# The first tick of the first pair in two parts of channels, and two filter copies moved to ScalarE

## The chip, the cores and the metric

The kernel runs on one core of a Trainium2 chip. Its work is done by five engines that run beside each other and wait for each other through semaphores: TensorE (PE in the profile, PEld for its weight loads), VectorE (DVE), ScalarE (ACT), GpSimd (POOL) and SyncE (SP). The last two mostly issue DMAs here. The metric is the time of one execution on the device in microseconds; shown is the median of several runs.

## The reference

Two steps are computed, on an input of 8 sequences, 5696 positions and 128 channels. First a causal convolution of every channel with a filter as long as the sequence, through a Fourier transform of twice the length. Then a mixing in frequency space: 64 modes of the result are multiplied by complex 128x128 matrices, transformed back and added, and a last 128x128 product with a ReLU is added to that.

```python
L = 2 * S
Xf = np.fft.rfft(x, n=L, axis=1)
Hf = np.fft.rfft(h, n=L, axis=0)
y = np.fft.irfft(Xf * Hf[None], n=L, axis=1)[:, :S, :]      # the convolution
X = np.fft.rfft(y, axis=1)[:, :64]
Y[:, :64] = X mixed by w_r + i w_i                           # 128x128 for each mode
u = y + np.fft.irfft(Y, n=S, axis=1)
out = u + np.maximum(u @ w_ch, 0.0)
```

## The kernel before, in words

The length 5696 is split into 89 times 64, so that each Fourier transform becomes two matrix products. The eight sequences are taken as four pairs (`g_` from 0 to 3); both sequences of a pair lie beside each other in 64 partitions each.

For a pair, the **first transform** comes as 32 tiles of four channels each (`a_tile`, line 462). PE writes a tile into two PSUM banks, and ScalarE or VectorE copies it out to the array `As` (tile token `("as", j)`); the last tile, 31, is copied half by each. The **second transform** (`second`, line 608) takes the 90 frequencies in 23 ticks of four, and writes one bank for each of the two sequences, all 128 channels of four frequencies in a bank. It takes the channels from `d0` to `d1`: with all of them it reads all tiles of `As`, with fewer it reads the tiles up to `d1` alone. The **products** with the filter (`products`, line 628) are made by VectorE into the buffers `U`. Normally ScalarE first copies the two banks into `Xs` (`copied`, line 588), and VectorE multiplies from there. Tick 0 has a form of its own: the first sequence is multiplied straight from PSUM, and the second is copied first by ScalarE (`copy_b`) and then multiplied (`first_u`, line 620). Two ticks behind, PE transforms `U` back (`Z`, matmuls with `Wc`, two of three banks 4, 5, 6 in turn), ScalarE copies it out and SP's queue stores it to DRAM; three ticks behind, PE adds up the modes in bank 7 (matmuls with `G`).

The **filter** goes through the same second transform, but once only, in the stage of the first pair. `filter_tick` (line 487) makes four frequencies of it in two banks, an engine copies them to `Hs`, and two DMAs on SP's queue write a copy with both halves of the partitions exchanged. Filter ticks 0 to 5 are spread among the tiles of the first transform (lines 739 to 743). From then on tick `t` of the first pair makes filter tick `t + 6`, in banks 2 and 3, as the last thing that the tick puts on PE (line 733). Line 503 says which engine copies a filter tick: ScalarE for ticks 0, 1, 3, 4 and 5, VectorE for all others.

The order of work on each engine is the order in which these functions are called, and each engine follows it strictly; waits are worked out from tokens (tiles, banks, buffers) by a recorder. Three calls of `keep` put matmuls on PE whose results nobody reads: 16 between the last tile of the first transform and tick 0 of the first pair (line 744), and 8 after each of ticks 0 and 1 of that pair (line 752).

Tick 0 lies in banks 6 and 7 in all pairs (`ZSLOT`, line 602). In the pairs from the second on, its second transform is already done in two parts. The first 116 channels (`DA`) of both sequences are put on PE right after the last tile of the first transform (line 765); the other 12 follow in tick 0 for the second sequence (line 646) and in tick 1 for the first sequence (lines 678 to 680). The first pair does it in one piece, at the beginning of tick 0 (line 677).

Of the kernel before, what the change touches and what calls it, by code (L numbers as in the profile page):

```python
# [123 lines left out]
def bass_long_conv_fft__then__afno_spectral_mix_kernel(nc, x, h, moe_w_r, moe_w_i, moe_w_ch, out):  # L124
    B, S, D = x.shape
# [25 lines left out]
    c, s = np.cos(th), np.sin(th)  # L151
# [137 lines left out]
    ps = nc.alloc_psum_tensor("ps", [P, 8 * 512], F32)  # L289
# [9 lines left out]
    def bank(i):  # L299
        return ("bank", i)  # L300
# [123 lines left out]

    W1, W2, WI = wc_sb[:, 0:P], wc_sb[:, P:2 * P], wi_sb[:, :]
    XSLOT = [0, 2]
    ZSLOT, DA = 6, 116
    ZBANK = [4, 5, 6]
    MB = 7
    WARM = 92  # L430
# [56 lines left out]
    def filter_tick(t, banks):  # L487
        n = len(ticks[t])
        hb = banks
        for i, k in enumerate(ticks[t]):  # L490
            for r in range(2):
                for dh in range(2):
                    mm(pv(hb[dh], i * DH, [[1, DH]]),
                       ap(m_sb, MW, J * dh, J, k * 3 * J + (J if r == 0 else 0) + dh * J, [[1, P]]),
                       ap(ah_sb, HW, J * dh, J, (2 * k + r) * DH, [[1, DH]]), r == 0, r == 1,
                       AHT + mtok(k) + [("ag", k)], [bank(hb[dh])])
        lo, hi = KT * t * D, (KT * t + n) * D
        old = once("xr", [t_ for r_ in XR for t_ in r_]) if t == 0 else []
        for i in range(NXH):
            if KT * t + n > KH[i // 2]:  # L500
                old = old + once(("xh", i), xtok(i))
        evac(h_sb[:, lo:hi], pv(hb[0], 0, [[DH, n], [512, 2], [1, DH]]), [bank(hb[0]), bank(hb[1])], [("h", t, 0)],
             eng="scalar" if t < LH and t != 2 else "vector",
             after=old)
        for p0, p1 in ((0, J), (J, 0)):
            dma("sync", h_sb[p0:p0 + J, HW + lo:HW + hi], h_sb[p1:p1 + J, lo:hi], "s", [("h", t, 0)], [("h", t, 1, p0)])
        if t % 2 and t // 2 < NG:
            s0, s1 = t // 2 * GP, min(t // 2 * GP + GP, NS)
            dma("sync", g_sb[:, s0 * P:s1 * P], bass.AP(c_g, s0 * P, [[GW, P], [1, (s1 - s0) * P]]), "c", (),
                [("g", t // 2)], after=[("ag", k) for k in range(s0, s1)])  # L510
# [90 lines left out]
    def slot_of(g_, t):  # L601
        if t == 0:
            return ZSLOT
        if g_ == 0:
            return XSLOT[(t + 1) % 2 if not with_h_at(g_, t) else 0]
        return XSLOT[((t - 1) // 4 + t) % 2]
# [13 lines left out]
    def first_u(b, s_, row, tok, d0, d1):  # L620
        n = len(ticks[0])
        R.add("vector", lambda e: e.tensor_tensor(  # L622
            bass.AP(u_s[0], b * 512 + d0, [[2048, P], [1024, 2], [D, n], [1, d1 - d0]]),
            bass.AP(s_[0], s_[1] + d0, [[row, P], [0, 2], [D, n], [1, d1 - d0]]),
            bass.AP(h_sb, d0, [[2 * HW, P], [HW, 2], [D, n], [1, d1 - d0]]), MULT),
              [tok, ("h", 0, 0), ("h", 0, 1, 0), ("h", 0, 1, J)], [("u", 0)])

    def products(g_, t, sl):
        n = len(ticks[t])
        bk = [bank(sl), bank(sl + 1)]  # L630
        i = t % NU
        hv = bass.AP(h_sb, KT * t * D, [[2 * HW, P], [HW, 2], [0, 2], [1, n * D]])
        uv = bass.AP(u_s[i], 0, [[2048, P], [1024, 2], [512, 2], [1, n * D]])
        src = pv(sl, 0, [[0, 2], [512, 2], [1, n * D]])
        if t == 0:
            e = turns("e", list(range(NXS)))
            def copy_b():
                evac(bass.AP(x_s[e], 512, [[1024, P], [1, n * D]]), pv(sl + 1, 0, [[1, n * D]]), [bank(sl + 1)], [("xs", e)], eng="scalar")

            if g_ == 0:  # L640
                copy_b()
                first_u(0, (ps, sl * 512), 4096, bank(sl), 0, D)
                first_u(1, (x_s[e], 512), 1024, ("xs", e), 0, D)
                return
            first_u(0, (ps, sl * 512), 4096, bank(sl), 0, DA)
            second(g_, 0, DA, D, (1,))
            copy_b()
            first_u(1, (x_s[e], 512), 1024, ("xs", e), 0, D)
            return
        if not straight(g_, t):  # L650
            e = onchip.get((g_, t))
            if e is None:
                e = copied(g_, t, sl)
            src, bk = bass.AP(x_s[e], 0, [[1024, P], [0, 2], [512, 2], [1, n * D]]), [("xs", e)]
        R.add("vector", lambda e: e.tensor_tensor(uv, src, hv, MULT),  # L655
              bk + [("h", t, 0), ("h", t, 1, 0), ("h", t, 1, J)], [("u", i)])
# [10 lines left out]
    def tick(g_, t):  # L667
        if g_ + 1 < NP:
            for i in range(2 * XC):
                if t == XPLACE[g_ > 0][i]:  # L670
                    x_place(i, bass.AP(x_room(g_ + 1, i), 0, [[XB, NQ], [D, XN], [1, D]]), xtok(i))
        with_h = with_h_at(g_, t)
        if t < NT:
            of_two = t > 0 and twin(g_, t - 1)
            if not of_two:
                if g_ == 0 or t:
                    second(g_, t)
                if g_ and t == 1:
                    second(g_, 0, DA, D, (0,))
                    first_u(0, (ps, slot_of(g_, 0) * 512), 4096, bank(slot_of(g_, 0)), DA, D)  # L680
            products(g_, t, slot_of(g_, t))
            if twin(g_, t):
                second(g_, t + 1)
                if straight(g_, t):
                    copied(g_, t + 1, slot_of(g_, t + 1))
        drain = list(border[t]) if t in border and g_ + 1 < NP else []
        if drain and t >= NT:
            j, sl, e = drain.pop(0)
            a_tile(j, [sl], e)
        if g_ + 1 < NP:  # L690
            i = t // 2 - 1 if t % 2 == 0 else -1
            if g_ == 0:
                i = XLATE.index(t) + NXH if t in XLATE else -1
            if 0 <= i < 2 * XC:
                x_load(g_ + 1, i, x_room(g_ + 1, i), xtok(i), [("u", t % NU)] + AST)
        if LC <= t < NT + LC:
            s_ = t - LC
            n = len(ticks[s_])
            i, zi = s_ % NU, zroom(g_, s_)
            zb = [turns("z", ZBANK) for b in range(2)]  # L700
            for b in range(2):
                for r in range(2):
                    mm(pv(zb[b], 0, [[1, n * D]]), (W1, W2)[r], u_s[i][:, r * 1024 + b * 512:r * 1024 + b * 512 + n * D],
                       r == 0, r == 1, [("u", i), ("wc",)], [bank(zb[b])])
                evac(bass.AP(z_s[zi], b * D, [[1024, P], [2 * D, n], [1, D]]),
                     pv(zb[b], 0, [[D, n], [1, D]]), [bank(zb[b])], [("zs", zi, b)], eng="scalar",
                     after=once(("zx", zi, b), Z_OLD) if zi >= NZ else ())
            zo = (g_ * NK + KT * s_) * P * 256
            dma("sync", bass.AP(zs, zo, [[256, P], [P * 256, n], [1, 256]]),
                bass.AP(z_s[zi], 0, [[1024, P], [256, n], [1, 256]]), "z",  # L710
                [("zs", zi, 0), ("zs", zi, 1)], [("zd", g_, s_)])
            if drain and t >= NT:
                j, sl, e = drain.pop(0)
                a_tile(j, [sl], e)
        if LM <= t < NT + LM:
            s_ = t - LM
            zi = zroom(g_, s_)
            for i, k in sorted(enumerate(ticks[s_]), key=lambda q: (s_ > 0 or q[1] != 1, q)):
                for b in range(2):
                    if k % 2:  # L720
                        o, off, n, sl = pv(MB, b * P, [[1, P]]), (k + 1) // 2 * P, P, (k + 1) // 2
                    else:
                        ms, off = even[k]
                        n, sl = 2 * len(ms), 0
                        dims = [[M, 2]] if len(ms) == 1 else [[ms[1] - ms[0], 2], [M, 2]]
                        o = pv(MB, b * P + ms[0], dims)
                    mm(o, z_s[zi][:, i * 256 + b * P:i * 256 + b * P + P], g_sb[:, off:off + n],
                       k == 1 and b == 0, k == NK - 1 and b == 1, [("g", sl // GP), ("zs", zi, b)], [bank(MB)])
        if drain and t < NT + LM - 1:
            j, sl, e = drain.pop(0)  # L730
            a_tile(j, [sl], e)
        if with_h:
            filter_tick(t + LH, [2, 3])
# [5 lines left out]
    for j in range(32):  # L739
        a_tile(j, FOUR, "both" if j == 31 else SHARE[j])  # L740
        if j >= 11 and j % 3 == 2 and (j - 11) // 3 < LH:
            h_ = turns("s", FOUR)
            filter_tick((j - 11) // 3, [h_, h_ + 1])
    keep(16, turns("s", FOUR))
    for g_ in range(NP):
        if g_ == NP - 1:
            load_w(0)
# [216 lines left out]
```

## Time and profile before

| | |
|---|---|
| runs shown, median (lowest to highest) | 378.18 us (377.16 to 381.03) |
| profiled execution, its own time | 379.06 us |
| span of the profiled execution | 377.3 us |
| mean granted TensorE clock | 0.995 |
| busy PE, ACT, DVE, POOL (share of the span) | 95%, 83%, 78%, 20% |
| first transform of the first pair and filter ticks 0 to 5 | about 27 to 43 us |
| ticks of the first pair | about 44 to 92 us |
| one whole later pair | 54.5 us |
| last stage, results and output | about 252 to 377 us |

The table is read from the page and from the busy times by stretches. The durations of the profile come from one execution, so they add up to its own time and not to the median. A line such as L323 is that of a helper through which all matmuls go; tiles tell what an instruction does: `ps<-F,Xin` is the first transform, `ps<-As,M` the second, `ps<-Ah,M` the filter's, `ps<-F` alone the matmuls of `keep`, `U<-..,Hs` a product, `Hs<-ps` the copy of a filter tick, and `Xs<-ps` the copy ahead of a product.

### The profile page before, as it was taken

What the parts mean: (1) busy time and instruction counts of PE and PEld (TensorE: products, weight loads), DVE (VectorE), ACT (ScalarE), POOL (GpSimd) and SP (SyncE); (2) the same over time, 40 slices, a digit from 0 to 9 for tenths busy, and PEclk for the clock granted to TensorE, in tenths of its full rate; (3) what the DMA queues carried; (4) which work ended last, traced back from release to release, by engine and by line L of the source; (5) the groups of instructions that cost most, each with busy time, mean ns of one, the idle gap of its engine ahead of it and who ended that gap; (6) DMA issues with size and microseconds to landing.
All of it is one profiled execution on the core that took longest, in us unless ns stands there. A gap on an engine that the chain in (4) does not pass through costs nothing.

```text
span 377.3 us, 12488 instructions
## 1 busy us (share of the span) xinstructions
PE 359.0 (95%) x5370; PEld 279.0 (74%) x5370; DVE 295.1 (78%) x336; ACT 314.7 (83%) x495; POOL 75.4 (20%) x117
## 2 busy tenths in 40 slices
PE   7989989999999999999999999999999999999994
PEld 7878856666866666866667856667899989888873
DVE  3548889998898999998998988873547767756666
ACT  8468779998999997989997999996557677688885
POOL 8803011200552320743220401124000000000000
PEclk9998999999999999999999999999999999999999
DMA  7999959987899997899996899999999999999978
GB/s 145 209 289 363 242 148 200 264 214 225 130 159 197 221 265 221 95 144 207 256 261 178 85 292 344 336 364 351 366 408 394 414 418 407 414 404 384 362 303 343
DMA packets 87048, 103.94 MB, mean 276 GB/s; under 512 B 22730, under 2 KB 72522, under 8 KB 83438
## 3 DMA queue, kind: packets, MB, share of 16 engines
q1 hardware_dynamic: 64610, 81.33, 61.3%
q0 software_dynamic: 22384, 21.83, 35.0%
q8 instruction: 42, 0.69, 0.7%
q14 instruction: 12, 0.10, 0.1%
HBM read 70.61 MB, written 51.12 MB: 323 GB/s over the span
## 4 chain that ended last, share of the span: by engine, by line
PE 60%; ACT 15%; DMA 9%; DVE 7%; issue 4%; POOL 3%; SPq 1%; DVEq 0%; ACTq 0%; POOLq 0%
PE ps L323 60%; ACT As L313 7%; DMA out_dram<-O 4%; DMA Xr<-in_x_dram 4%; ACT Zs L311 2%; DVE As L317 2%; ACT Xs L311 2%; POOL Xr L320 2%; ACT Zt L311 2%; ACT R L896 1%; DMA Hs<-Hs 1%; DVE Xin L365 1%; POOL Hin L320 1%; DVE U L655 1%; DVE U L622 1%
## 5 line engine op out<-in xcount | busy, mean ns | idle before, releaser
L655 DVE TENSOR_TENSOR U<-Xs,Hs 128x2048 f16<-128x2048 f16 (+1 forms) x73 | 86.6, 1192 | 13.9 <-ACT Xs L311 12.9
L323 PE MATMUL ps<-U,Wc 128*128 128x512 f16 (+1 forms) x368 | 94.0, 376 | 1.4 <-DVE U L622 1.4
L311 ACT CAST Xs<-ps 128x1024 f16<-128x1024 f32 (+1 forms) x77 | 74.8, 978 | 9.9 <-PE ps L323 6.9
L311 ACT CAST Zs<-ps 128x512 f16<-128x512 f32 (+1 forms) x132 | 69.1, 594 | 1.7 <-PE ps L323 1.7
L897 DVE TENSOR_TENSOR O<-ps,R 128x512 f32<-128x512 f32 x81 | 52.3, 684 | 20.7 <-ACT R L896 11.3
L317 DVE TENSOR_SCALAR As<-ps 128x720 f16<-128x720 f32 (+1 forms) x67 | 55.8, 881 | 6.7 <-PE ps L323 5.2
L896 ACT ACTIVATE R<-ps 128x512 f32<-128x512 f32 (+1 forms) x92 | 50.5, 591 | 8.7 <-PE ps L323 8.6
L323 PE MATMUL ps<-F,Xin 128*128 128x180 f16 x512 | 53.5, 254 | 3.9 <-DVE Xin L365 2.4
L323 PEld LDWEIGHTS ps<-F,Xin 128*128 128x128 f16 x512 | 45.8, 155 | 11.2 <-DVE As L317 3.3
L323 PE MATMUL ps<-As,M 64*128 64x128 f16 (+2 forms) x1488 | 51.9, 215 | 1.3 <-ACT As L313 1.2
L313 ACT ACTIVATE As<-ps 128x720 f16<-128x720 f32 (+1 forms) x65 | 46.1, 768 | 8.2 <-PE ps L323 7.6
L323 PE MATMUL ps<-WI,UT 128*128 128x256 f16 x360 | 50.9, 278 | 0.5 <-ACT UT L311 0.4
L323 PEld LDWEIGHTS ps<-U,Wc 128*128 128x128 f16 x368 | 28.6, 97 | 30.3 <-ACT Zs L311 3.7
L311 ACT CAST UT<-ps 128x712 f16<-128x712 f32 x46 | 34.5, 752 | 18.2 <-PE ps L323 17.0
L323 PEld LDWEIGHTS ps<-As,M 64*128 64x128 f16 x1488 | 41.6, 94 | 7.6 <-ACT As L313 1.7
L323 PEld LDWEIGHTS ps<-WI,UT 128*128 128x128 f16 x360 | 39.0, 152 | 3.4 <-issue 1.8
L323 PE MATMUL ps<-IBs,C 128*128 128x356 f16 x128 | 39.2, 314 | 0.5 <-DVE O L897 0.4
L320 POOL DMA_DIRECT2D Xt<-in_x_dram x40 | 21.5, 542 | 80.5 <-PE ps L323 80.0
L323 PEld LDWEIGHTS ps<-G,Zs 128*128 128x128 f16 x512 | 26.1, 96 | 14.5 <-ACT Zs L311 2.0
L655 DVE TENSOR_TENSOR U<-ps,Hs 128x2048 f16<-128x2048 f32 x15 | 34.3, 2284 | 0.0
L323 PE MATMUL ps<-G,Zs 128*128 128x128 f16 (+2 forms) x512 | 32.2, 192 | 0.1
L311 ACT CAST Zt<-ps 128x512 f16<-128x512 f32 x52 | 28.5, 622 | 0.2 <-PE ps L323 0.2
(74 smaller groups left out, 483.1 us busy)
## 6 DMA issues: line engine op xcount, KB each, us to landing
out_dram<-O SPq DMA_DIRECT2D x39, 512.0 KB, 9.9
zscr<-Zs SPq DMA_DIRECT2D x62, 256.0 KB, 6.1
zscr<-Zt SPq DMA_DIRECT2D x26, 256.0 KB, 6.3
Xt<-in_x_dram POOLq DMA_DIRECT2D x20, 320.0 KB, 7.0
W<-wscr SPq DMA_DIRECT2D x4, 1024.0 KB, 7.7
ZT0a<-zscr SPq DMA_DIRECT2D x4, 1024.0 KB, 10.3
M<-cM POOLq DMA_DIRECT2D x5, 720.0 KB, 16.8
ZT1a<-zscr SPq DMA_DIRECT2D x3, 1024.0 KB, 11.0
```

The lines of the kernel that those rows point to most:

```text
L311: R.add(e, lambda h_: h_.copy(dst, src), reads, writes, after=after)
L313: R.add(e, lambda h_: h_.activation(dst, src, COPY, scale=scale), reads, writes, after=after)
L317: R.add(e, lambda h_: h_.tensor_scalar_mul(dst, src, scale), reads, writes, after=after)
L320: R.add(eng, lambda h_: h_.dma_start(dst, src), reads, writes, ring=ring, after=after)
L323: R.add("tensor", lambda h_: h_.matmul(o, l, r, start=st, stop=sp), reads, writes)
L365: R.add("vector", lambda e: e.tensor_copy(bass.AP(x_sb, i * XN * XS, [[XW, NQ], [XS, XN], [1, D]]), src), list(toks) + XZ, [("xin", i)])
L622: R.add("vector", lambda e: e.tensor_tensor(bass.AP(u_s[0], b * 512 + d0, [[2048, P], [1024, 2], [D, n], [1, d1 - d0]]), bass.AP(s_[0], s_ ...
L655: R.add("vector", lambda e: e.tensor_tensor(uv, src, hv, MULT), bk + [("h", t, 0), ("h", t, 1, 0), ("h", t, 1, J)], [("u", i)])
L896: R.add("scalar", lambda e: e.activation(rv, src_r, RELU), bk, [("r", i % NR)], after=once(("r", i % NR), G_ALL + XTT + [("y", 0), ("y", 1 ...
L897: R.add("vector", lambda e: e.tensor_tensor(ov, src_u, rv, ADD), bk + [("r", i % NR)], [key + (h_,)], after=once(key, old))
```

## The change

Three things change, all at the beginning of the first pair. The 16 matmuls of `keep` before tick 0 go, and in their place stands the second transform of tick 0 for the first 120 channels (`DF`), which reads tiles 0 to 29. The remaining 8 channels follow as in the later pairs: for the second sequence in tick 0, behind the first product, and ahead of ScalarE's copy; for the first sequence in tick 1, behind that tick's own transform, with a small product of their own ahead of tick 1's product. And the copies of filter ticks 6 and 7 go from VectorE to ScalarE. The order of the two operations on the second sequence's bank and the first product is that of the later pairs: product first, copy after it; they are on different engines.

```diff
-    ZSLOT, DA = 6, 116
+    ZSLOT, DA, DF = 6, 116, 120
...
-             eng="scalar" if t < LH and t != 2 else "vector",
+             eng="scalar" if t < LH + 2 and t != 2 else "vector",
...
-            if g_ == 0:
-                copy_b()
-                first_u(0, (ps, sl * 512), 4096, bank(sl), 0, D)
-                first_u(1, (x_s[e], 512), 1024, ("xs", e), 0, D)
-                return
-            first_u(0, (ps, sl * 512), 4096, bank(sl), 0, DA)
-            second(g_, 0, DA, D, (1,))
+            d_ = DA if g_ else DF
+            first_u(0, (ps, sl * 512), 4096, bank(sl), 0, d_)
+            second(g_, 0, d_, D, (1,))
             copy_b()
             first_u(1, (x_s[e], 512), 1024, ("xs", e), 0, D)
...
-                if g_ == 0 or t:
+                if t:
                     second(g_, t)
-                if g_ and t == 1:
-                    second(g_, 0, DA, D, (0,))
-                    first_u(0, (ps, slot_of(g_, 0) * 512), 4096, bank(slot_of(g_, 0)), DA, D)
+                if t == 1:
+                    d_ = DA if g_ else DF
+                    second(g_, 0, d_, D, (0,))
+                    first_u(0, (ps, slot_of(g_, 0) * 512), 4096, bank(slot_of(g_, 0)), d_, D)
...
-    keep(16, turns("s", FOUR))
+    second(0, 0, 0, DF)
```

## The prediction

> **What bounds the kernel now.** The page comes first, for the whole, and then the busy times by stretches around the change. The columns of a stretch are its length, then busy time (instructions) of PE, PEld, DVE, ACT and POOL, granted TensorE clock, DMA share, GB/s.
>
> ```profile
> span 377.3 us, 12488 instructions
> PE 359.0 (95%) x5370; PEld 279.0 (74%) x5370; DVE 295.1 (78%) x336; ACT 314.7 (83%) x495; POOL 75.4 (20%) x117
> ...
> 43.20:49.10 5.90, 4.70 (x100) 4.01 (x99) 4.65 (x7) 2.74 (x4) 0.00 (x0) 1.00 0.75 209
> 55.00:79.00 24.00, 23.95 (x517) 16.24 (x518) 23.55 (x28) 22.50 (x35) 4.32 (x8) 1.00 0.97 223
> ```
>
> The average (PE 95%) hides the place: in the steady ticks of the first pair (55 to 79 us) PE, DVE and ACT are all full, while in the six microseconds where the first pair begins (43.2 to 49.1) PE has 4.70 us of work in 5.90 and ACT 2.74. That place is read instruction by instruction: the last evacuations of the first transform, and then the timeline (start, duration, engine, line, operation, out<-in).
>
> ```profile
> 42.88 0.90 DVE L317 TENSOR_SCALAR As<-ps 128x720 f16<-128x720 f32 x1
> 43.80 0.55 ACT L313 ACTIVATE As<-ps 128x360 f16<-128x360 f32 x1
> ...
> 43.32 1.26 PEld L323 LDWEIGHTS ps<-F 128*128 128x128 f16 x16
> 44.73 0.45 PEld L323 LDWEIGHTS ps<-As,M 64*128 64x128 f16 x16
> 45.13 0.33 PEld L323 LDWEIGHTS ps<-Ah,M 64*128 64x128 f16 x16
> 45.39 1.22 DVE L622 TENSOR_TENSOR U<-ps,Hs 128x1024 f16<-128x1024 f32 x1 [1.15 <-PE ps L323]
> 45.42 0.59 ACT L311 CAST Xs<-ps 128x512 f16<-128x512 f32 x1 [1.08 <-PE ps L323]
> 45.51 0.58 PEld L323 LDWEIGHTS ps<-F 128*128 128x128 f16 x8
> 46.24 0.45 PEld L323 LDWEIGHTS ps<-As,M 64*128 64x128 f16 x16
> 46.72 0.69 DVE L622 TENSOR_TENSOR U<-Xs,Hs 128x1024 f16<-128x1024 f16 x1
> 46.91 1.01 ACT L311 CAST Xs<-ps 128x1024 f16<-128x1024 f32 x1 [0.90 <-PE ps L323]
> 47.33 0.68 DVE L315 CAST Hs<-ps 128x512 f16<-128x512 f32 x1
> 48.06 0.29 PEld L323 LDWEIGHTS ps<-Ah,M 64*128 64x128 f16 x16 [1.37 <-DVE Hs L315]
> 48.40 0.58 PEld L323 LDWEIGHTS ps<-F 128*128 128x128 f16 x8
> 49.12 0.45 PEld L323 LDWEIGHTS ps<-As,M 64*128 64x128 f16 x16
> 49.79 1.01 ACT L311 CAST Xs<-ps 128x1024 f16<-128x1024 f32 x1 [1.87 <-PE ps L323]
> 50.84 1.22 DVE L655 TENSOR_TENSOR U<-Xs,Hs 128x2048 f16<-128x2048 f16 x1 [1.06 <-ACT Xs L311]
> ```
>
> Two losses are to be seen. First, tile 29 of the first transform is out of PSUM at 42.88+0.90 = 43.78 and the last half of tile 31 at 43.80+0.55 = 44.35, but the second transform of tick 0 starts at 44.73, behind 16 fill matmuls that last past both. Second, PE stands 1.37 us before filter tick 7 (48.06): banks 2 and 3 are free only when DVE has copied filter tick 6 (47.33 to 48.01), and DVE does that after its two products of tick 0. Everything after it follows from that: the transform of tick 2 at 49.12, its ScalarE copy at 49.79, its product at 50.84.
>
> Some ticks later the chain that ended last runs into PE and stays there for a long way:
>
> ```profile
> 55.05 23.93 PE ps L323 x516
> ```
>
> So what is won at tick 2 is won for all that follows, if nothing behind it is tied to a fixed time.
>
> **The change part by part.** I follow PE's own order with durations from these rows; a semaphore passes in about 0.05 (48.01 to 48.06). The same split into a large and a small part stands in the trace for the second pair, with 116 and 12 channels, and prices the forms which the first pair doesn't have yet:
>
> ```profile
> 106.35 0.42 PEld L323 LDWEIGHTS ps<-As,M 64*128 64x128 f16 x16
> 107.00 1.11 DVE L622 TENSOR_TENSOR U<-ps,Hs 128x928 f16<-128x928 f32 x1
> 107.32 0.65 PEld L323 LDWEIGHTS ps<-As,M 64*128 64x128 f16 x24 [0.55 <-ACT As L313]
> 107.72 2.43 ACT L311 CAST Xs<-ps 128x512 f16<-128x512 f32 x3 [0.44 <-PE ps L323]
> 109.13 0.26 DVE L622 TENSOR_TENSOR U<-ps,Hs 128x96 f16<-128x96 f32 x1
> ...
> L311 ACT CAST Hs<-ps 128x512 f16<-128x512 f32 x5 | 2.9, 581 | 0.0
> L315 DVE CAST Hs<-ps 128x512 f16<-128x512 f32 x17 | 11.6, 682 | 0.0
> ```
>
> *Removed: 16 fill matmuls.* They take 44.73-43.32 = 1.41 us of PE. Only what lies past the new wait is a gain.
>
> *Large part (16 matmuls of 120 channels).* It needs tiles 0 to 29; tile 28 is out before 29, so the wait ends at 43.78+0.05 = 43.83 in place of 44.73. Its 16 weight loads take 0.42 (row of 116 channels; 0.45 with 128), to 44.25. The first product on DVE begins 0.65 after the start (107.00-106.35), at 44.48, not 45.39. With 960 elements it lies between 1.11 (928) and 1.22 (1024); I take 1.15, to 45.63.
>
> *Small part, second sequence (8 matmuls of 8 channels).* This is the added wait: for tile 31, 44.35+0.05 = 44.40, so PE stands 0.15 us, with filter tick 6, 8 fill matmuls and the transform of tick 1 queued behind it. The price of 8 such matmuls is not in a row of its own: 24 weight loads took 0.65 at 107.32, so 0.22 for 8; between nothing (if they hide behind the neighbours) and 0.42 (as 16 large ones) I take 0.23, to 44.63. The ScalarE copy starts 0.40 after their start (107.72-107.32): 44.82 to 45.41, in place of 45.42.
>
> *Tick 0's remainder.* Filter tick 6 takes 0.38 on PE (45.13 to 45.51) and the 8 fill matmuls 0.73 (45.51 to 46.24): 44.63 to 45.01 to 45.74. The second product on DVE waits for both its copy (45.41) and the first product: 46.72 minus the end of the first, 46.61, is 0.11, so 45.74 to 46.43.
>
> *Tick 1.* Its transform starts at 45.74 (46.24 before) and takes 0.42 with more 64-row matmuls behind it. The small part of the first sequence then writes bank 6, which the first product left at 45.63, so it waits for nothing: 46.16 to 46.39 by the same 0.23. DVE's piece for it (64 elements; at most the 0.26 of 96) starts near 46.55 and ends near 46.8, beside idle time: the next DVE work, tick 1's product, waits for its copy on ScalarE, which starts 0.67 after the transform (46.91-46.24), 46.41, and ends 47.42.
>
> *The two filter copies on ScalarE.* Each is 0.58 there and 0.68 on DVE. Filter tick 6's is queued behind the copy of tick 0 (45.41), so it ends near 45.99, ahead of the copy of tick 1, whose data come at 46.41: no cost. Banks 2 and 3 are free at 45.99, and PE arrives at filter tick 7 at 46.39: the stall of 1.37 is gone. Filter tick 7's copy on ScalarE stands between the copies of tick 1 and tick 2: 47.42 to about 48.0; tick 2's data come at 48.17, so it hides with 0.17 to spare. Without that cover it would delay tick 2's copy by what it overlaps, at most its 0.58. Both copies' swaps (two DMAs each on SP's queue) go out earlier by the same steps; nothing is moved past them, and their data are read six ticks later.
>
> *Tick 2.* PE: filter tick 7 from 46.39, 0.34 (48.06 to 48.40), fill 0.72 (48.40 to 49.12), so the transform of tick 2 could start at 47.45; banks 0 and 1 are free at 47.42+0.05 = 47.47. I take 47.50 against 49.12. Its product on DVE follows 1.72 after it (50.84-49.12), at 49.22, and DVE is idle by then (tick 1's product from 47.45, 1.22). From here each instruction has the same predecessors and the same distances as before. **The sum: 49.12-47.50 = 1.62 us.** What is late next is PE's own order (two sets of 8 fill matmuls, 1.45 us in all) level with the ScalarE copy of tick 1.
>
> *What could hold the shift up.* The first placing of the next pair's input (DVE, tick 3) moves to about 51; its loads land by 31.2+14.5 = 45.7:
>
> ```profile
> L320 POOL DMA_DIRECT2D Xh<-in_x_dram x8: 515/528/551, 27.6 to 31.2; - x8
> DMA to landing us min/median/max: 10.2/12.0/14.5
> ```
>
> The later pairs' loads and the weights' rewriting are issued after tiles or products, so they shift too. The last stage is full on both sides:
>
> ```profile
> 265.00:323.00 58.00, 58.00 (x878) 51.83 (x876) 37.42 (x54) 39.06 (x64) 0.00 (x0) 1.00 1.01 402
> ```
>
> DMA share 1.01 there, but its loads wait for the last pair's results, so the full stretch begins earlier by the same 1.62.
>
> **From the profiled execution to the number.** It took 379.06 us, 377.3 of span and 1.76 around it; by the sum 377.4. It lies 0.9 above the median of the runs, 378.18 (377.16 to 381.03), so I put the gain on the median: **376.6 us**.
>
> **The rivals.** (1) *The large part waits for all tiles after all*, so the change does only part of what it says: start 44.40 and not 43.83. The transform of tick 1 then starts at about 46.1, its copy ends at 47.8, the transform of tick 2 starts at 47.9: gain 1.2, 377.0 us. Against it: the code asks for tiles 0 to 29, and the bank's last reader is tile 29.
>
> (2) *The gain is given back later*, because the saturated stretch at 402 GB/s sets the end from a transfer that doesn't move: 378.2. For it speaks the DMA share of 1.01; against it, that I find no transfer there with a fixed start.
>
> (3) *Slower: the clock.* The fill matmuls taken out kept PE occupied, and the trace shows what a gap can cost:
>
> ```profile
> 24.90:28.30 3.40, 1.66 (x22) 1.47 (x20) 1.74 (x3) 0.28 (x1) 0.71 (x2) 1.00 1.02 400
> 28.30:31.70 3.40, 3.33 (x25) 3.17 (x24) 2.40 (x4) 2.73 (x4) 3.40 (x7) 0.56 1.02 422
> 45.40:48.80 3.40, 2.20 (x59) 1.78 (x52) 3.30 (x4) 1.60 (x2) 0.00 (x0) 1.00 0.63 186
> ```
>
> After a stretch of 3.40 us with 1.66 busy the granted clock averaged 0.56 over the next 3.40 us; the loss is 3.40x0.44 = 1.50 us of full clock. Around 44 us, where PE is on the path, one such event takes back nearly all of the gain, and two (43 to 50 us) give 378.18-1.62+3.00 = 379.6. It decides from about half a stretch idle. Against it: the kernel before has 2.20 busy of 3.40 at 45.40 to 48.80 and keeps 1.00, and the new order has under 0.6 us idle there (43.4 to 43.83, 44.25 to 44.40). [...]
>
> **How the numbers follow.** Forecast 0.78, rival 1 0.08, rival 2 0.07, rival 3 0.07. The unknown prices (first product 1.11 to 1.22, small parts 0 to 0.42 each, the copy of filter tick 7 hidden or not) put the gain between 1.1 and 1.9. With the lowest run, 377.16-1.9 = 375.3, and for medians a little lower still 375.2; upwards the range takes in rivals 1 and 2 with some scatter of the median above 378.2, to 378.8. One per cent, about what a measurement of this kernel can tell from no change, is 3.8 us, more than twice the gain: within 1% 0.93, faster by more 0.03, slower by more 0.04 (three clock events, or a median as high as the highest run).
>
> **What would show it.** After the change: matmuls of 64x120 from about 43.8 and a DVE product of 128x960 from 44.5; 7 filter copies of 128x512 on ACT and 15 on DVE; no PE wait of over 0.3 us for a filter copy between 45 and 50; the transform of tick 2 at about 47.5, its product at 49.2; the steady stretch of the chain, at 55.05 now, at 53.4; and every later stage 1.6 earlier, with the same durations. Wrong would be: DVE waiting for the input's DMA near 51, ACT's filter copy ahead of a copy that was ready, a granted clock below 1.00 after 43 us, or later stages that are no longer 1.6 ahead.

## The result, and the profile after

The kernel after takes **377.2 us** (median of 22 runs, 376.75 to 379.14); the kernel before, run beside it, 378.33 (22 runs, 377.16 to 381.03). The ratio is 0.9969, with a 95% interval of 0.9954 to 0.9983: 1.17 us won, between 0.64 and 1.74. By the bound of one per cent that is no change, as forecast; the gain is real, for the interval leaves out 1, and it is smaller than the 1.62 of the sum. The time lies 0.6 above the 376.6 of the prediction and inside its range. That range, 375.2 to 378.8, would have held with no gain at all, so the number says little for the mechanism; the traces have to show that.

The page of the kernel after, and its busy times by the same stretches as before (length, then busy time and instructions of PE, PEld, DVE, ACT and POOL, granted clock, DMA share, GB/s):

```profile
span 376.1 us, 12494 instructions
...
PE 357.8 (95%) x5370; PEld 278.1 (74%) x5370; DVE 294.3 (78%) x335; ACT 315.7 (84%) x497; POOL 75.0 (20%) x117
```

```profile
43.20:49.10 5.90, 5.54 (x126) 4.19 (x128) 4.45 (x6) 4.76 (x9) 0.00 (x0) 1.00 0.87 240
55.00:79.00 24.00, 24.00 (x518) 16.28 (x515) 22.71 (x28) 23.01 (x36) 3.35 (x6) 1.00 1.00 229
```

The place of the change fills up: PE has 5.54 us of work in the 5.90 where it had 4.70, and ScalarE 4.76 where it had 2.74. In the steady ticks behind it the DMA share goes from 0.97 to 1.00.

The timeline of the kernel after, at the same place (start, duration, engine, line, operation, out<-in, idle time before it and releaser):

```profile
44.03 0.74 PE L323 MATMUL ps<-As,M 64*128 64x120 f16 x21 [0.36 <-DVE As L317]
44.64 1.16 DVE L622 TENSOR_TENSOR U<-ps,Hs 128x960 f16<-128x960 f32 x1 [0.30 <-PE ps L323]
44.88 0.58 ACT L311 CAST Xs<-ps 128x512 f16<-128x512 f32 x1 [0.44 <-PE ps L323]
45.37 0.59 ACT L311 CAST Hs<-ps 128x512 f16<-128x512 f32 x1
46.42 1.01 ACT L311 CAST Xs<-ps 128x1024 f16<-128x1024 f32 x1 [0.47 <-PE ps L323]
46.70 0.23 DVE L622 TENSOR_TENSOR U<-ps,Hs 128x64 f16<-128x64 f32 x1
46.74 0.58 PEld L323 LDWEIGHTS ps<-F 128*128 128x128 f16 x8
47.33 0.59 ACT L311 CAST Hs<-ps 128x512 f16<-128x512 f32 x1
47.49 0.45 PEld L323 LDWEIGHTS ps<-As,M 64*128 64x128 f16 x16 [0.17 <-ACT Xs L311]
48.15 1.01 ACT L311 CAST Xs<-ps 128x1024 f16<-128x1024 f32 x1 [0.23 <-PE ps L323]
49.20 1.23 DVE L651 TENSOR_TENSOR U<-Xs,Hs 128x2048 f16<-128x2048 f16 x1 [0.51 <-DMA Hs<-Hs]
```

The transform of tick 2 starts at 47.49 (49.12 before, 47.50 forecast), its product at 49.20 (50.84 before, 49.22 forecast). The copy of filter tick 6 ends at 45.96 on ScalarE, and the wait of 1.37 us before filter tick 7 is gone. Up to here the working stands step by step.

Behind it the lead melts. The chain that ended last, in the kernel before and then in the kernel after (start, length, engine, what):

```profile
109.45 27.27 PE ps L323 x430
164.00 27.27 PE ps L323 x430
218.57 33.33 PE ps L323 x524
```

```profile
53.41 19.59 PE ps L323 x428
75.22 4.92 DMA Hs<-Hs
107.96 27.27 PE ps L323 x430
162.54 27.27 PE ps L323 x430
190.98 7.35 DMA Xt<-in_x_dram
198.35 0.70 DVE Xin L365
217.36 33.33 PE ps L323 x524
```

The steady stretch begins at 53.41, 1.64 earlier than the 55.05 of before. Then PE's long run ends after 19.59 us, and transfers stand on the chain: at 75.22 a swap of the filter, at 190.98 a load of input. The second pair is 1.49 ahead, the third 1.46, the fourth 1.21, and the span ends 1.2 earlier.

The first of these losses in the timeline of the kernel after, around the product of tick 16:

```profile
71.84 2.06 SPq L320 DMA_DIRECT2D Hs<-Hs  x2
76.16 1.22 DVE L651 TENSOR_TENSOR U<-Xs,Hs 128x2048 f16<-128x2048 f16 x1
77.19 1.01 ACT L311 CAST Xs<-ps 128x1024 f16<-128x1024 f32 x1
79.19 1.23 DVE L651 TENSOR_TENSOR U<-Xs,Hs 128x2048 f16<-128x2048 f16 x1 [1.21 <-ACT Zs L311]
```

VectorE stands 1.21 us before the product at 79.19. By the code it waits for the ScalarE copy that it reads, which ended at 77.19+1.01 = 78.20, and for filter tick 16 with both swapped halves; the copy of `Zs` that the row names isn't among its conditions. What came last is the swapped half: its two DMAs were issued from 71.84 on, and the second landed at 79.10 by the trace's DMA events. (Releasers are inferred from semaphore events, and this row's is not the one.)

### The profile page after: what moved, and what is told of

It is laid out like the page before. It is cut to its first block, busy times and chain, and to the rows that moved or that the text cites. A ratio compares the mean times of both kernels' runs of the same rounds, so it can differ in the third digit from the quotient of the medians.

```text
span 376.1 us, 12494 instructions
## 1 busy us (share of the span) xinstructions
PE 357.8 (95%) x5370; PEld 278.1 (74%) x5370; DVE 294.3 (78%) x335; ACT 315.7 (84%) x497; POOL 75.0 (20%) x117
## 4 chain that ended last, share of the span: by engine, by line
PE 67%; ACT 11%; DMA 10%; DVE 5%; issue 3%; POOL 3%; SPq 0%; DVEq 0%; POOLq 0%
PE ps L323 67%; ACT As L313 7%; DMA Hs<-Hs 4%; DMA Xr<-in_x_dram 4%; DVE As L317 2%; DMA Xt<-in_x_dram 2%; POOL Xr L320 2%; ACT Zs L311 1%; ACT R L893 1%; POOL Hin L320 1%; DVE Xin L365 1%; ACT Xs L311 1%; DVE U L622 1%; DVE Hs L315 1%; ACT Zt L311 1%
## 5 line engine op out<-in xcount | busy, mean ns | idle before, releaser
L323 PE MATMUL ps<-As,M 64*128 64x128 f16 (+3 forms) x1504 | 52.3, 214 | 2.1 <-ACT As L313 1.3
L311 ACT CAST UT<-ps 128x712 f16<-128x712 f32 x46 | 34.5, 752 | 17.8 <-PE ps L323 16.8
```

Source lines behind the costliest of these rows:

```text
L311: R.add(e, lambda h_: h_.copy(dst, src), reads, writes, after=after)
L323: R.add("tensor", lambda h_: h_.matmul(o, l, r, start=st, stop=sp), reads, writes)
```

## The experiments

**How they are read.** Times of single executions scatter by more than a microsecond (376.75 to 379.14 in the kernel after), so beside the ratio each trace gives a *lead*: how much earlier than in the trace of before a product of the first pair (tick in the column's head) or the first product of pair 2 or 4 starts, or the span ends, both counted from the end of tile 29's copy. That takes out what happened ahead of the change. It is needed: in some executions (five of the fourteen traces) the granted clock falls at 28 us, to a mean of 0.52 to 0.58 over 28.3 to 31.7 us, long before the changed part, and the tile then ends at 43.5 to 43.9 and not at 42.1 to 42.6. Two cautions go with it. A later event whose place doesn't move with the tile cuts the lead of a trace without the fall by more, since that trace gets there up to 1.7 us sooner. And all leads are taken against one trace of the kernel before; its own second trace, e8_before_again, differs from it by up to 0.26 in the columns and by 0.38 at the end, so smaller differences mean nothing. All numbers in us.

```
                        tick 2  tick 5  tick 12  tick 16  tick 18  pair 2  pair 4   end
after                    1.74    1.74    1.92     0.96     1.61     1.60    1.32    1.27
e1_again                 1.74    1.74    1.72     0.71     1.35     1.35    0.97    1.02
e10_third                1.75    0.43    0.02     0.01     0.12     0.12   -0.17    0.23
e2_split_only            0.91    0.57   -0.37    -0.37    -0.26    -0.27   -1.05   -1.03
e3_scalar_only           1.16    1.00    1.18     0.76     0.87     0.87    0.83    0.49
e4_no_fill               0.35    0.35    0.30    -1.05    -0.41    -0.42   -0.59   -0.03
e5_no_keeps              2.30    2.02    2.20     1.05     1.40     1.40    1.39    1.52
e9_no_keeps_again        2.31    2.31    1.95     1.95     2.05     2.05    1.67    1.95
e6_swap_pool             1.75    0.70    0.29     0.29    -0.56    -0.56   -0.60   -2.31
e7_no_keeps_swap_pool    2.31    2.01    2.27     2.27     2.38     2.38    2.38    2.88
e8_before_again         -0.01    0.00    0.03    -0.26    -0.16    -0.16   -0.18    0.38
e11_xh_later             1.75    0.71    0.81     0.79     0.90     0.90    0.43    0.79
e12_no_keeps_xh_later    2.30    2.30    2.48     1.29     1.39     1.40    0.84    1.29
```

### The change again, and its two halves

The kernel after once more, and each half of the change alone.

```diff
 # e2_split_only, on the kernel after
-             eng="scalar" if t < LH + 2 and t != 2 else "vector",
+             eng="scalar" if t < LH and t != 2 else "vector",
 # e3_scalar_only, on the kernel before
-             eng="scalar" if t < LH and t != 2 else "vector",
+             eng="scalar" if t < LH + 2 and t != 2 else "vector",
```

> The changed kernel once more, unchanged. All theories: the transform of tick 2 about 1.63 us earlier than in the kernel before (47.49 against 49.12 in the first pair of traces). Theory A (part of the gain is lost at fixed places: the 1.2 us that DVE waits at the product of tick 16, and the last input load of the third pair): the same two waits at the same places again, and the last stage again only 1.2 ahead. Theory B (those losses are chance events of one execution): they are absent or elsewhere, and the lead at the last stage lies between 1.2 and 1.8. Time against before: 0.9957 to 0.997 under both.

> The split of tick 0 and the removal of the 16 fill matmuls, but filter ticks 6 and 7 still copied by VectorE. By my steps: the large part at 43.83, the VectorE copy of filter tick 6 behind both products, 46.35 to 47.03, filter tick 7 on PE at 47.08 after a stall of 0.69, the transform of tick 2 at 48.14: 0.98 earlier than before, ratio about 0.9974. Rival (the stall ahead of filter tick 7 is the only loss, so the split alone buys nothing): transform of tick 2 within 0.2 of 49.12, ratio 1.000.

> Only the copies of filter ticks 6 and 7 moved to ScalarE; the 16 fill matmuls and the single second transform of tick 0 stay. By my steps: filter tick 7 on PE at 46.66 with no stall, the transform of tick 2 held by ScalarE's copy of tick 1, at 47.97: 1.15 earlier, ratio about 0.997. So the two parts alone add up to 2.13, more than the 1.63 of both together. Rival (the parts are independent, 1.63 minus 0.98): 0.65 earlier, ratio 0.9983.

Measured: e1_again 377.58 us, ratio 0.9988 (0.9968 to 1.0009); e2_split_only 377.79, 0.9986 (0.9963 to 1.0008); e3_scalar_only 377.55, 0.9978 (0.9966 to 0.9991). At tick 2 the split alone is worth 0.91 and the copies alone 1.16. Together they would be 2.07; both shorten the same wait for a time, and the whole gives 1.74 in three traces out of three. So the start of the mechanism is settled to a tenth of a microsecond. What follows isn't: each of these traces loses lead again, at different places. In e1_again it is the swap of tick 16 again, landing 0.08 us before its product. In e2_split_only PE itself stands, for no reason that the trace names:

```profile
49.27 0.45 PE L323 MATMUL ps<-As,M 64*128 64x128 f16 x9 [0.35 <-issue]
68.86 0.26 PE L323 MATMUL ps<-Ah,M 64*128 64x64 f16 x6 [0.95 <-issue]
```

"issue" is idle time in which the engine waits for no event that the trace has.

### The fill matmuls

e4_no_fill takes only the 16 fill matmuls out of the kernel before and leaves tick 0 as it was. e5_no_keeps takes the two sets of 8 out of the kernel after, and e9_no_keeps_again is the same kernel on another chip. No result reads these matmuls.

```diff
 # e4_no_fill, on the kernel before
-    keep(16, turns("s", FOUR))
 # e5_no_keeps and e9_no_keeps_again, on the kernel after
-            if g_ == 0 and t < 2:
-                keep(8, 4)
```

> The kernel before without the 16 fill matmuls ahead of tick 0, nothing else changed. By my steps the second transform of tick 0 starts 0.05 after the last half of tile 31 is out, 0.33 earlier than behind the fill, and everything after it by the same: lead at tick 2 0.33, ratio about 0.999. Clock rival: without the fill the granted clock falls somewhere between 43 and 55 us, at a price of about 1.5 us, ratio 1.003.

> The changed kernel without the two sets of 8 fill matmuls after ticks 0 and 1. By my steps: the transform of tick 1 moves from 45.76 to 45.03, the small part of the first sequence then waits for the first product (45.80), ScalarE's copy of tick 1 is queued behind that of filter tick 6 and ends near 46.92, so the transform of tick 2 starts at 46.97: another 0.52, 2.15 in all, ratio about 0.9943 to 0.9955. Clock rival: PE is then idle for about 1.4 us of 3.4 near 45; if that is enough to lower the granted clock (as after the stretch with 1.66 of 3.40 busy), one such event costs about 1.5 us, the granted clock between 45 and 52 is well under 1.00 and the ratio is about 0.998 or more.

> The changed kernel without the two sets of 8 fill matmuls, once more, beside the changed kernel on the same chip. Distance from the end of tile 29's copy to the product of tick 2 as before, 4.76 us (5.32 in the changed kernel, 7.06 in the kernel before). If the 0.56 that this saves at tick 2 is worth what it is at the end, the ratio is about 0.0015 below that of the changed kernel; if the wait for the swap at tick 16 takes it all back, the two are alike. Granted clock 1.00 from 45 to 52 us, against the clock rival.

Measured: e4_no_fill 377.58, 0.9983 (0.9962 to 1.0003), 0.35 ahead at tick 2; so 0.35 of the split's 0.91 is fill that stood in the way. e5_no_keeps 376.02, **0.9943 (0.9923 to 0.9963)**; e9_no_keeps_again 376.39, **0.9951 (0.9933 to 0.9969)**. Both are ahead by 2.3 at tick 2: the two sets of 8 cost 0.56 of path. These runs bear on the rival of the clock too, and go further than the change does. The stretch of e5_no_keeps in which no fill is left:

```profile
45.00:52.00 7.00, 6.38 (x136) 4.13 (x138) 6.27 (x8) 6.31 (x11) 0.94 (x2) 1.00 0.73 191
```

PE is idle for 0.62 us of 7.00 and the granted clock is 1.00. It is 1.00 between 43 and 52 us in all fourteen traces. At this place the clock doesn't need the fill. The rival's own condition, about half a stretch idle, was not reached, though: the emptiest 3.40 us from 42 us on still hold 2.26 us of TensorE's work in e5 and e9 and 2.14 in e4, against the 1.66 of the rival's row. What a deeper gap would do here is not shown.

### The swaps on another queue

A filter tick's copy is swapped by two DMAs that SP's queue issues between the stores of `Zs`. If the product waits because SP comes late to them, another queue must remove the wait; if the DMA engines are simply full, it must not. The swaps of filter ticks 6 to 22 go to GpSimd's queue, on the kernel after (e6_swap_pool) and on e5_no_keeps (e7_no_keeps_swap_pool). GpSimd's queue gets a ring of eight semaphores of its own for them. The kernel before was run once more beside them (e8_before_again).

```diff
-            dma("sync", h_sb[p0:p0 + J, HW + lo:HW + hi], h_sb[p1:p1 + J, lo:hi], "s", [("h", t, 0)], [("h", t, 1, p0)])
+            dma("gpsimd" if t >= LH else "sync", h_sb[p0:p0 + J, HW + lo:HW + hi], h_sb[p1:p1 + J, lo:hi],
+                "r" if t >= LH else "s", [("h", t, 0)], [("h", t, 1, p0)])
```

> The changed kernel, with the swaps of filter ticks 6 to 22 issued by GpSimd's queue and not by SP's. In the traces of the changed kernel the product of tick 16 starts 0.08 us after the swap of filter tick 16 lands (79.10), and SP issues that swap only at 71.84, 4.3 us after its copy is done. Theory Q (SP's queue is behind): the swaps are issued within a microsecond of their copies, the swap of tick 16 lands some 4 us ahead of its product, no product waits for one, and the lead of 1.74 at tick 2 is still there at tick 18 (1.35 to 1.61 in the changed kernel); ratio about 0.996. Theory D (the DMA engines themselves are full, share 1.00 at 55 to 79 us): issued earlier, the swaps still land late; the smallest distance from landing to product stays below 1 us, and the ratio stays at 0.997 to 0.999.

> The changed kernel without the two sets of 8 fill matmuls, and with the swaps of filter ticks 6 to 22 on GpSimd's queue. The lead at tick 2 is 2.30 as without the fill. Theory Q: it is kept to tick 18 (1.40 there with the swaps on SP's queue), ratio about 0.992. Theory D: it shrinks to about 1.4 again, ratio about 0.9943 as before.

> The kernel before once more, unchanged, for a second trace. In the first one the granted clock fell to 0.56 at 28.3 to 31.7 us and the first transform ended at 43.78; in three traces of later kernels it didn't fall and that stage ended 1.45 earlier. If this is a chance event of an execution, the code up to there being the same, the stage ends at 43.8 with a fall and at 42.3 without; the distance from the end of tile 29's copy to the product of tick 2 is 7.06 in both cases. If the kernel before always has the fall, 43.8 again. Ratio 1.000.

Measured: e6_swap_pool 378.5, 1.0002 (0.998 to 1.0024); e7_no_keeps_swap_pool 376.74, 0.9975 (0.9955 to 0.9996); e8_before_again 378.3, 1.0004 (0.998 to 1.0028). The swap of one filter tick, from the trace's DMA events:

```
                              copy ended  first issued  both landed  product starts  to spare
before, tick 16                 69.22        72.83         79.92         80.05         0.13
before, tick 17                 71.55        75.50         82.25         82.33         0.08
after, tick 16                  67.58        71.84         79.10         79.19         0.08
e6_swap_pool, tick 16           67.47        67.76         74.00         78.12         4.13
e7_no_keeps_swap_pool, tick 16  65.85        66.59         73.26         76.50         3.24
```

On SP's queue the swap is issued 3.6 to 4.3 us after its copy; on GpSimd's 0.3 to 0.7. From there to landing it is 6.2 to 7.3 us in all five rows. With the other queue no product waits for a swap (1.6 us to spare at the least in both traces), and e7 carries its lead of 2.3 to the fourth pair, with a dip of 0.3 made good. With SP's queue at least one product starts 0.08 us after its swap has landed in eight of the twelve traces: at tick 16 in the kernel after, e1, e4 and e5, at 13 in e3, e5 and e12, at 14 in e3, at 17 in the kernel before and in e2. So the wait comes from SP's queue being behind. Whether it bites in a given execution hangs on the landing as well: in e2, e9, e10 and e11 the swap of tick 16 is issued 2.5 to 3.6 us after its copy, lands within 3.7 to 5.1, and has 3.1 to 4.0 to spare. The time doesn't follow: e6 lost its lead to PE's nameless waits (below), and the executions of both kernels lie far apart (376.32 to 379.79, and 374.95 to 378.75; the traced one was e6's slowest and e7's fastest). In e6 another 1.7 us went after the fourth pair, in the last stage. What GpSimd's queue costs there was not looked for.

### PE's waits without a releaser

e10_third is the kernel after a third time. e11_xh_later and e12_no_keeps_xh_later move the early loads of the second pair's input behind tile 20 of the first transform, to see whether something that PE needs comes earlier then.

```diff
-    for i in range(NXH):
-        x_load(1, i, x_h[i], xtok(i), [t_ for r_ in XR for t_ in r_])
+        if j == 20:                      # in the loop over the tiles
+            for i in range(NXH):
+                x_load(1, i, x_h[i], xtok(i), [t_ for r_ in XR for t_ in r_] + [("as", j)])
```

> The changed kernel a third time. Distance from the end of tile 29's copy to the product of tick 2: 5.32. If the lead of 1.74 at tick 2 is cut by waits whose place is set by the DMA queues, the lead at tick 18 is again between 1.3 and 1.7 with a product that starts within 0.1 us of a swap's landing, or with a gap on TensorE whose releaser the profile doesn't show; ratio 0.996 to 0.999. If the first two traces were unlucky, the full 1.74 stands at tick 18.

> The changed kernel, with the four early loads of the second pair's input issued after tile 20 of the first transform (about 38 us) and not at 27.6. Theory F (in executions without the fall of the clock, the lead of 1.74 is cut by a fixed time: the block of TensorE's instructions that begins at its weight load 605 is fetched only when the backlog of early loads has drained, packet at 46.1 to 46.5 us in every trace so far, and TensorE goes on at 48.9 to 49.3): the packet comes earlier than 46, there is no gap of unknown releaser on TensorE at load 605, and the lead at tick 5 is that at tick 2, 1.74. Rival (that packet's time has nothing to do with the loads): it stays at 46.1 to 46.5, and the gap of 0.4 to 1.5 us is there unless the clock fell. In both the moved loads can make VectorE wait at about 50 us, which would show as a wait for a DMA at the first placing.

> The same move of the four loads, in the changed kernel without the two sets of 8 fill matmuls. Theory F: lead at tick 2 2.30 and at tick 5 the same 2.30 (2.02 before the move, without a fall of the clock), ratio about 0.993. Rival: tick 5 as before the move, ratio 0.9945 to 0.995.

Measured: e10_third 377.02, 0.9973 (0.9959 to 0.9988); e11_xh_later 377.12, 0.9977 (0.996 to 0.9995); e12_no_keeps_xh_later 376.06, 0.9958 (0.9938 to 0.9977). Three traces of the same kernel after now stand side by side, and e10_third loses 1.32 of its lead of 1.75 between ticks 2 and 5. PE's timeline in it:

```profile
47.53 0.38 PE L323 MATMUL ps<-As,M 64*128 64x128 f16 x7
49.24 0.45 PE L323 MATMUL ps<-As,M 64*128 64x128 f16 x9 [1.33 <-issue]
49.62 0.61 PE L323 MATMUL ps<-U,Wc 128*128 128x512 f16 x2
```

Sixteen matmuls of one transform, nothing between them to wait for, and PE stops for 1.33 us after the seventh. And in e6_swap_pool:

```profile
48.96 0.45 PE L323 MATMUL ps<-As,M 64*128 64x128 f16 x9 [1.06 <-issue]
61.83 0.21 PE L323 MATMUL ps<-Ah,M 64*128 64x64 f16 x2 [0.41 <-issue]
81.51 0.34 PE L323 MATMUL ps<-As,M 64*128 64x128 f16 x6 [0.83 <-issue]
```

Counting PE's weight loads from 0 at the start of the program, such a stop comes ahead of number 605 (e2, e5, e6, e7, e10, e11; one later in e3), 861 (e6), 989 (e2, e9, e10), 1117 (e3) and 1245 (e6): always 605 plus a multiple of 128, whichever instruction stands there (at 605 a second transform in e2, e6, e10 and e11, the mode sum with `G` in e5 and e7). One weight load and one matmul go together (5370 of each on the page), so 128 loads are 256 instructions. The page has a queue that fits:

```profile
q8 instruction: 42, 0.69, 0.7%
```

42 packets with 0.69 MB are 16.4 KB each, and 42 times 128 is 5376, against 5370 weight loads in all. Counted back from 605 the borders are load 93 and every 128th after it, which makes 42 too, and taken in order each packet starts within 6 us of TensorE's passing of its border, with a median of 2.6 to 3.0 us behind it. So I read the row, as an estimate from these counts and times alone, as TensorE's instructions in blocks of 256, each brought by a transfer of its own that starts about one border ahead. The packet that goes with border 477 (passed at 42.5 to 44.3), and by this reading brings the block from load 605 on, starts between 46.1 and 46.8 in every trace but e12 and takes 0.9 to 1.2 us; in the seven traces with a stop there PE goes on between 48.86 and 49.31, 1.4 to 1.6 us after the packet's end. In the kernel before PE gets to load 605 only at 51.01 and 49.87 (two traces), in the kernel after at 49.37 and 49.09 where the clock had fallen, and none of these stops; in e10 the load ahead of it starts at 47.64. Such a crossing cost up to 1.33 us (e10_third).

So there is a nearly fixed time after all, near 49 us, and the change brings PE up against it in the executions in which the clock didn't fall and the first transform ended early. What sets the packet's time is not settled. The guess was that it waits until the early loads of the second pair's input have drained (issued at 27.6 to 31.2, landing by 45.7 in the kernel before). With them moved, the packet came at 46.77 and at 47.36, not earlier, and e11 still stopped:

```profile
49.05 0.45 PE L323 MATMUL ps<-As,M 64*128 64x128 f16 x9 [1.05 <-issue]
```

That refutes a packet that waits for the last of the loads, for in these two traces they land only by 51.3 and 52.9. It does not clear the loads: issued from 37.6 and 39.1 on, they are in flight at 46 us as before, so the move didn't empty the queues there. At the border before, where it lowered the DMA share, it speaks for the guess. The packet that goes with border 349 starts 2.9 to 3.7 us behind it in the twelve traces with the early loads at 27 us, and 0.6 behind it in both with the loads moved; from 34.5 to 38 us the DMA share is 1.05 in the kernel after, 0.69 in e11 and 0.48 in e12. No run has the loads out of the way at 46 us.

The two sets of 8 fill matmuls stand ahead of load 605, so without them the border lies 16 matmuls further on in the work. The load ahead of it then starts at 48.50 in e5 and 48.78 in e7, and the stop is 0.36 and 0.30, against 1.33, 1.06 and 1.05 in e10, e6 and e11, where that load starts at 47.6 to 47.7.

In e12 the clock fell, PE came later and didn't stop; it lost 1.3 at the swap of tick 13 on SP's queue instead (0.08 us to spare).

## Why the prediction was right, and where it wasn't

**The start, right.** Large part, added wait, small parts, first product, the two copies on ScalarE: the forms that had no row of their own came out as bounded. The kernel after by groups (line, engine, operation, count | busy, mean ns | idle before):

```profile
L622 DVE TENSOR_TENSOR U<-ps,Hs 128x960 f16<-128x960 f32 x1 | 1.2, 1158 | 0.3 <-PE ps L323 0.3
L622 DVE TENSOR_TENSOR U<-ps,Hs 128x64 f16<-128x64 f32 x1 | 0.2, 226 | 0.1
L315 DVE CAST Hs<-ps 128x512 f16<-128x512 f32 x15 | 10.2, 681 | 0.0
L311 ACT CAST Hs<-ps 128x512 f16<-128x512 f32 x7 | 4.1, 583 | 0.0
```

1.16 us against 1.15 for the first product, 0.23 against at most 0.26 for the small one, 7 and 15 copies. The added wait and the start of the large part moved by 0.1 to 0.2, all hidden behind what was forecast to be late next: the transform of tick 2 waits 0.17 us for ScalarE's copy of tick 1, level with PE's own order. The sum of 1.62 is 1.64 at the product of tick 2 (50.84 to 49.20); counted from tile 29's copy, which ended 0.10 later in the kernel after (43.88), it is 1.74. One slip of the sum is without effect: ScalarE's copy of tick 0 starts at 44.40+0.40 = 44.80 by its own terms, not 44.82.

**The step that failed** is the one that carried the 1.62 to the end: "From here each instruction has the same predecessors and the same distances as before", with "their data are read six ticks later" for the swaps. The predecessors are the same; the distances of the transfers are not. Three things took lead back:
- The swaps. Six ticks are some 12 us, but SP comes to the swap of tick 16 only 4.3 us after the copy and its landing takes 7.3 more. The kernel before already had only 0.13 and 0.08 us to spare at ticks 16 and 17 in the trace that the prediction was made from (2.46 and 0.46 in its second). Tick 16 cost 0.95 of lead, of which 0.65 came back by tick 18; some 0.2 of that, at tick 17, stands in the other traces too, e8_before_again among them, and so belongs to the trace of before.
- PE's stops at the borders of its instruction blocks: up to 1.33 at load 605 (e10_third), in executions that get there early.
- The last load of the fourth pair's input, on the chain at 190.98: 1.56 ahead becomes 1.32; in e9 2.03 becomes 1.67.

Measured by the medians, the term "1.62 for all that follows" is 1.17 (0.64 to 1.74) in the first comparison, 0.45 (-0.34 to 1.21) and 1.02 (0.45 to 1.55) in the other two of the same kernel, worked out as one minus the ratio, times the time before. How much each of the three takes in the average execution can't be said from single traces: three of the same kernel end 1.27, 1.02 and 0.23 ahead, and one of the unchanged kernel 0.38. By their spans the traces with the fall of the clock are 1.2 apart (377.27 before, 376.10 and 376.07 after), those without it 0.3 (375.74 before, 375.42 after). That fits a gain which these stops cut mainly where the clock didn't fall, but it rests on five executions.

**The rivals.** (1) The large part doesn't wait for all tiles: its row names VectorE's copies as the releaser, and at 44.03 it starts behind that of tile 29 (out at 43.88) and ahead of the end of both halves of tile 31 (44.34 and 44.44). (2) Part of the gain was given back later, which was this rival's thought, but not at its place: the last stage is full on both sides, with DMA share 1.01, and in the kernel after it keeps what it gets (1.32 at the fourth pair, 1.27 at the end). In the other two traces of the kernel after the last stage adds 0.05 and 0.40 to the lead. (3) The clock: 1.00 in the kernel after from 43 us until 373.6, when TensorE has finished, and 1.00 between 43 and 52 us in e5 and e9, where none of the three sets of fill matmuls is left. The rival's "about half a stretch idle" was read from one row, and it was not enough there: near 28 us seven traces hold 3.41 us with 1.59 busy or less and kept 1.00.

**A version that beats both kernels** is the kernel after without the two sets of 8 fill matmuls. On each of the three chips where it or its variant e12 ran beside the kernel after or its variant e11, its median is lower: 376.02 against 377.58, 376.39 against 377.02, 376.06 against 377.12. Against the kernel before, the two comparisons give 0.6% and 0.5% less time.

## What to carry to other kernels

A lead won at the head of a long chain is worth what the tightest transfer behind it lets through (0.13 and 0.08 us to spare in the trace of before; 1.74 us of lead at tick 2, 0.96 at tick 16): list, from more than one trace of before, by how much each buffer's transfer lands ahead of its reader, and take the lead off that, before "the same distances" is believed. A transfer issued right behind its copy in the program may be issued microseconds later on a queue that also serves stores (3.6 to 4.3 us here, against 0.3 to 0.7 on GpSimd's queue). Matmuls that only keep an engine occupied are priced by taking them out, and where the work around them fills the engine, they are on the path (0.56 us here for two sets of 8).

## What the runs showed of the hardware

**PE stopped at borders of 256 instructions.** It stands for up to 1.33 us (e10_third, weight load 605) in the middle of a row of equal matmuls, shown as idle time for "issue"; eight of fourteen traces have at least one such stop in the first pair. That its supply of instructions is what it waits for is the reading above: 42 packets of 16.4 KB on the queue named "instruction", and at load 605 PE goes on 1.4 to 1.6 us after the end of one.

**The clock's fall at 28 us is not decided by the busy share alone.** The same stretches in the kernel after, and in e8_before_again:

```profile
24.90:28.30 3.40, 1.33 (x17) 1.14 (x15) 1.70 (x3) 0.18 (x1) 0.61 (x2) 1.00 1.02 386
28.30:31.70 3.40, 3.33 (x26) 3.16 (x24) 2.40 (x4) 2.83 (x4) 3.40 (x7) 0.58 1.01 422
```

```profile
24.90:28.30 3.40, 1.58 (x21) 1.39 (x19) 1.71 (x3) 0.20 (x1) 0.62 (x2) 1.00 1.02 395
28.30:31.70 3.40, 3.33 (x37) 2.95 (x35) 3.27 (x5) 3.40 (x6) 3.40 (x7) 1.00 1.01 422
```

After 1.33 us busy the clock falls to 0.58, after 1.58 it stays at 1.00; but before had 1.66 busy and fell to 0.56. Five of the fourteen traces fell, four different programs among them; TensorE's work is the same in all fourteen up to this point. The stretches above begin at a set time, and the fall doesn't: it starts at 28.1 to 28.8 and lasts 3.41 us, and in the 3.41 us just ahead of it TensorE was busy for 1.39 to 1.59. Of the nine traces without a fall seven have 3.41 us at this place that hold no more than 1.59, and kept 1.00; the other two have 1.88 and 1.96 in their emptiest. So no fall came without a stretch about half idle, and such a stretch wasn't enough. The stretches ahead of the five falls hold 1.8 to 2.0 us idle, the 3.41 less those 1.39 to 1.59. What else decides it is not shown.
